# TensorE's order in an attention stage: from the planner's to one written out tile by tile

## The chip, the core and the metric

The kernel runs on one core of one Trainium2 chip. The metric is the device time of one execution in microseconds (us). A core has TensorE (PE in the rows; its weight loads are PEld), VectorE (DVE), ScalarE (ACT), GpSimd (POOL) and SyncE (SP, which issues nearly all DMAs here). Each engine works through its own instructions in order and waits for others by semaphores.

## What is computed

Clustered attention (2 batches, 8 heads, 768 rows, head size 64) followed by two MLPs over 1536 tokens of width 512, all in float32:

```python
q_assign = argmax(q_n @ c_n.T)      # 16 clusters a head; k_assign likewise
mask = q_assign[:, :, :, None] == k_assign[:, :, None, :]
scores = where(mask, scale * q @ k.T, -1e9)
attn = softmax(scores)
x = (attn @ v), heads side by side  # 1536 x 512
x = silu-like(x @ w_in) @ w_out     # 512 -> 2048 -> 512
out = (sigmoid(x @ w_gate) * (x @ w_val)) @ w_out2   # 512 -> 1536 -> 512
```

## The kernel before

Heads go in pairs p = 0 to 7 (two heads j = 0, 1 in each). A head's 768 query rows are 6 tiles of 128 rows, so a pair has 12 tiles, numbered 0 to 11 here (tile = 6 j + i). For each tile the kernel does the following.

- `scores` (L437): four matmuls into a PSUM tile s, two with the values (ka, qa) and two with the masking rows (k, q). DVE then takes the negated row maximum nm (L450) and ACT the exponential e with its row sums (L455). Each s takes two PSUM banks and there are two of them, so the scores of tile n+2 can start only when e of tile n is done.
- `transposes` (L463): six 128 x 128 transposes of e. Two go into u, which two tiles share and DVE copies once for two tiles (L475); four go into t (L478), copied by DVE for even and by ACT for odd tiles (L480). All copies land in one SBUF ring ph. The PSUM pool for u and t, `ps_t`, has three banks and also serves pm, ps, pt and pr below.
- `values` (L482): for each group of three tiles, twelve matmuls v over the ring with 64-column weights (L486), which run in two column halves of the array. ACT copies one half (`other`, L495) and DVE adds it to the other (`xf`, L498). A pair has groups 0 to 3 (tiles 0-2, 3-5, 6-8, 9-11).

Beside this, `prep(p + 1)` (L368) makes the next pair ready in eight pieces, one at each `yield`: 1 POOL scales and splits q; 2 POOL splits k, twelve DMAs place the parts, PE makes the cluster products pm (L151, 32-column weights), ACT scales them; 3 PE transposes them (ps, L162), ACT copies; 4 DVE maximum (L406); 5, 6 DVE compares and weighs (L409, L412); 7 DVE L414 and L416 (oh); 8 PE transposes oh (pt, L425), ACT writes `rows` (L427), four DMAs carry them into the masking rows of the next pair (L429, L430). For pair 0, `first_masks` (L335) stands ahead of it with three pieces of its own, the last with a pt at L319. `finish(p)` (L500) normalizes a finished pair: DVE adds and inverts the sums (L504, L506), PE transposes them (pr, L508), ACT copies (L510); in later steps two DMAs spread them over the partitions (L576 to L579), POOL multiplies (acc, L516), and after pair 3 POOL goes on to make operands of the first MLP (L530, L65, L75). The last pair ends with `finish_last` (L552).

The order of the work in attention comes from the loop at L594: at step n it traces the values of the group that ended with tile n - 4, the scores of tile n + 2, pieces of prep, and the transposes of tile n. All engines are then placed by the framework's planner (outside of `manual_schedule` blocks), which may move an instruction ahead of others by its own estimates. Only the start of the kernel (`first`, L179) and TensorE's order in the MLPs (`order`) are written out by hand:

```python
LOOK, LAG = 2, 4
for n in range(len(tiles) + LAG):
    if n >= LAG: ... values(pp_, jj, ii // GT)
    if n < len(tiles): ... scores(*tiles[n + LOOK]); next(nxt, None); transposes(p, j, i)
```

During the last pair, weights for the first MLP are converted from two 32-bit words (`converted`, L649): ACT L658, POOL L659, DVE L664, L666, L668, each DVE step behind one of the last pair's row maxima.

Of the kernel before, what the change touches and what calls it, by code (L numbers as in the profile page):

```python
# [31 lines left out]
def clustered_attention_then_two_mlps(ctx, tc, qT, kT, v, cen, cenT, w1i, w1o, w2g, w2v, w2o, out):  # L32
    nc = tc.nc
    B, HP, _, S = qT.shape
# [4 lines left out]
    NT = S // P  # L39
# [5 lines left out]
    NPAIR = B * HP  # L45
# [3 lines left out]
    GT = G // P  # L49
# [8 lines left out]
    maxima = []  # L58
# [49 lines left out]
    with ExitStack() as att:  # L108
# [19 lines left out]
        def after_masks(p):  # L128

            return tc.issue_after(masked[p].ins) if p in masked else nullcontext()  # L130

        def load(p):
            b, hp = divmod(p, HP)
            qq = raw.tile([P, S], F32, tag="qq", name=f"qq{p}")
            kk = raw.tile([P, S], F32, tag="kk", name=f"kk{p}")
            vv = hd[p % 2].tile([P, 2, NT, D], F32, tag="vv", name=f"vv{p}")
            with after_masks(p - 1):
                nc.sync.dma_start(qq, qT[b, hp])
                nc.sync.dma_start(kk, kT[b, hp])
                loaded[:] = [nc.sync.dma_start(vv, v[b, hp])]  # L140
            raws[p] = (qq, kk, vv)
# [176 lines left out]
        def choice_rows(pt, j, i, at):  # L318
            nc.tensor.transpose(pt[0:D, at * P : (at + 1) * P], oh[0][:, i, j].rearrange("p n c -> p (n c)"), identb)  # L319
# [15 lines left out]
        def first_masks():  # L335
            yield from first_choice(1, sums)
            pt = ps_t.tile([P, 1024], BF16, tag="t", name="pt0_1")
            for i in range(NT):
                choice_rows(pt, 1, i, i)
            query_rows(1, pt, 0, 0, NT // 2)  # L340
            key_rows(nc.vector, 1, pt, 0, 0, NT)
            query_rows(1, pt, NT // 2, NT // 2, NT // 2)
            yield
# [7 lines left out]
        with tc.issue_after(cast(nc.gpsimd, mine, chosen.pop()).ins):  # L351
            with tc.issue_after(zeros(0, 1).ins):
                late = nc.gpsimd.tensor_tensor(km[U, 1], kk[U], kh[U], op=ALU.subtract)
# [83 lines left out]
        def scores(p, j, i):  # L437
            qa, qm, ka, km, _ = heads[p]
            s = ps_s.tile([P, 2, 512], F32, tag="s", name=f"s{p}_{j}_{i}")
            for n, (a, c) in enumerate(((qa, ka), (qm, km))):  # L440
                for g in range(2):
                    nc.tensor.matmul(  # L442
                        s[:, g, 0:HS],
                        lhsT=a[:, j, i * P : (i + 1) * P],
                        rhs=c[:, j, g * HS : (g + 1) * HS],
                        start=n == 0,
                        stop=n == 1,
                    )
            nm = sm.tile([P, 1], F32, tag="nm", name=f"nm{p}_{j}_{i}")
            maxima.append(nc.vector.tensor_reduce(nm, s[:, :, 0:HS], axis=AX.XY, op=ALU.max, negate=True))  # L450
            e = wk.tile([P, 2, HS], F32, tag="e", name=f"e{p}_{j}_{i}", bufs=4)
            if p not in tots:
                tots[p] = fin.tile([P, 2 * NT], F32, tag="tot", name=f"tot{p}")
            n = j * NT + i
            x = nc.scalar.activation(e, s[:, :, 0:HS], AF.Exp, bias=nm, scale=1.0, accum_out=tots[p][:, n : n + 1])  # L455
            if (p, j, i) == (NPAIR - 1, 0, 0):
                begin.append(x)
            prob[p, j, i] = e
# [4 lines left out]
        def transposes(p, j, i):  # L463
            e = prob.pop((p, j, i)).rearrange("p a b -> p (a b)")
            if i % 2 == 0:
                shared[0] = ps_t.tile([P, 2, 2, P], F32, tag="t", name=f"u{p}_{j}_{i}")
            both = shared[0]
            for kt in (4, 5):
                nc.tensor.transpose(both[:, kt - 4, i % 2, :], e[:, kt * P : (kt + 1) * P], ident)  # L469
            if i % 2:  # L470
                cast(
                    nc.vector,
                    ring[:, 4:6, (i - 1) * P : (i + 1) * P],
                    both.rearrange("p k i q -> p k (i q)"),
                )  # L475
            t = ps_t.tile([P, 4, P], F32, tag="t", name=f"t{p}_{j}_{i}")
            for kt in range(4):
                nc.tensor.transpose(t[:, kt, :], e[:, kt * P : (kt + 1) * P], ident)  # L478
            eng = nc.scalar if i % 2 or (p == NPAIR - 1 and i) else nc.vector
            cast(eng, ring[:, 0:4, i * P : (i + 1) * P], t)  # L480

        def values(p, j, g):  # L482
            vv = heads[p][4]
            o = ps_v.tile([P, G], F32, tag="v", name=f"v{p}_{j}_{g}")
            for n, kt in enumerate((4, 5, 0, 1, 2, 3)):
                m = nc.tensor.matmul(  # L486
                    o[(L, U)[kt % 2]],
                    lhsT=vv[:, j, kt, :],
                    rhs=ring[:, kt, g * G : (g + 1) * G],
                    start=n < 2,  # L490
                    stop=n >= NT - 2,
                )
            main, rest = (L, U) if j == 0 else (U, L)
            other = wk.tile([P, G], F32, tag="other", name=f"other{p}_{j}_{g}", bufs=1)
            ends[:] = [nc.scalar.activation(other[main], o[rest], AF.Copy), m]  # L495
            if p not in xf:
                xf[p] = fin.tile([P, S], F32, tag="xf", name=f"xf{p}")
            nc.vector.tensor_tensor(xf[p][main, g * G : (g + 1) * G], o[main], other[main], op=ALU.add)  # L498
# [53 lines left out]
        def finish_last(h):  # L552

            p = NPAIR - 1
            b, hp = divmod(p, HP)
            n = NT // 2
            t = tots[p].rearrange("p (j i) -> p j i", j=2)[:, :, h * n : (h + 1) * n]
            nc.vector.tensor_scalar_add(t, t, 1e-9)
            rs = fin.tile([P, 2, n], F32, tag="rs", name=f"rs{p}_{h}")
            nc.vector.reciprocal(rs, t)  # L560
            rb = ps_t.tile([P, 512], F32, tag="t", name=f"rb{p}_{h}")
            for j, r in enumerate((L, U)):
                for i in range(n):
                    nc.tensor.matmul(
                        rb[r, i * P : (i + 1) * P],
                        lhsT=rs[:, j, i : i + 1].to_broadcast([P, D]),
                        rhs=ident,
                        start=True,
                        stop=True,
                    )  # L570
            nc.vector.tensor_tensor(
                acc[:, hp, h, b, :], xf[p][:, h * HS : (h + 1) * HS], rb[:, 0:HS], op=ALU.mult
            )
# [7 lines left out]
        if NPAIR > 1:  # L581
            load(1)
        tiles = [(p, j, i) for p in range(NPAIR) for j in range(2) for i in range(NT)]
        LOOK, LAG = 2, 4
        for t in tiles[:LOOK]:
            scores(*t)
        warm(WARM[3])
        first.__exit__(None, None, None)
# [2 lines left out]
            zeros(1, 1)  # L591

        work = []
        for n in range(len(tiles) + LAG):  # L594
            if n >= LAG:
                pp_, jj, ii = tiles[n - LAG]
                if ii % GT == GT - 1:
                    values(pp_, jj, ii // GT)
            if n < len(tiles):
                p, j, i = tiles[n]  # L600
                later = tc.issue_after(maxima[1].ins) if n < 6 else nullcontext()
                if (j, i) == (0, 0):
                    nxt = prep(p + 1) if p + 1 < NPAIR else iter(())
                    if p == 0:
                        nxt = chain(first_masks(), nxt)
                if n + LOOK < len(tiles):
                    t = tiles[n + LOOK]
                    if t[1:] == (0, 0):
                        for _ in nxt:
                            pass  # L610
                        if p + 2 < NPAIR:
                            load(p + 2)
                    scores(*t)
                with later:
                    next(nxt, None)
                    if n < 6:
                        next(nxt, None)
                transposes(p, j, i)
            if n >= LAG:
                if pp_ == NPAIR - 1:  # L620
                    if jj == 1 and ii in (NT // 2, NT - 1):
                        finish_last(ii // (NT // 2 + 1))
                elif (jj, ii) == (1, NT - 1):
                    work.append(finish(pp_))
            work = [w for w in work if next(w, work) is not work]
        for w in work:
            for _ in w:
                pass


    wp = ctx.enter_context(tc.tile_pool(name="wp", bufs=3))
# [491 lines left out]
```

## Time and profile before

Times of whole executions and the page's busy times:

| what | us |
|---|---|
| median of 3 runs | 786.36 (785.64 to 789.41) |
| the profiled execution | 785.58 |
| its span, first to last instruction | 783.9 |
| PE busy in the span | 766.0 (98%) |
| DVE busy | 633.1 (81%) |
| ACT busy | 394.2 (50%) |
| POOL busy | 399.4 (51%) |
| granted TensorE clock | 1.000 of full speed |

The span holds the attention stage (to about 245 us), then the two MLPs. Busy PE is not PE at its peak: matmuls overlap, and the ends of matmuls are modelled, so distances between starts say more than durations. In a timeline row the number in square brackets is idle time before the instruction and what ended it.

### The profile page before, as it was taken

The numbers are of one execution on the slowest core, as the hardware profiler recorded it, in microseconds if no ns is written. First come the engines' busy times: TensorE is split into PE (matmuls) and PEld (weight loads), VectorE is DVE, ScalarE is ACT, GpSimd is POOL, SyncE is SP. The second block draws the span as 40 slices with busy tenths as digits, with TensorE's granted clock in tenths as the row PEclk, the third lists the DMA queues.
The fourth block names the chain that finished last, engine by engine and source line by source line (L and its number), as shares of the span: only waits on it lengthen the run. The fifth ranks groups of instructions, "written<-read, shape, count | busy, mean of one in ns | idle before, by whom it ended". The sixth has DMA issues, their size and how long they took to land.

```text
span 783.9 us, 11429 instructions
## 1 busy us (share of the span) xinstructions
PE 766.0 (98%) x4314; PEld 655.3 (84%) x4314; DVE 633.1 (81%) x803; ACT 394.2 (50%) x674; POOL 399.4 (51%) x345
## 2 busy tenths in 40 slices
PE   8999999999989999999999999999999999999998
PEld 4666766777757998989989989998998989999896
DVE  7786987887886989978688678998497896979746
ACT  6666766666767755525425236546532425333220
POOL 5324123457565756746446326445664846848220
PEclk9999999999999999999999999999999999999999
DMA  7764566467321132221221121211121221111004
GB/s 214 177 160 122 144 162 148 116 162 183 95 74 55 54 108 97 93 80 64 72 81 55 60 75 54 81 57 61 45 82 54 81 81 54 54 67 69 1 0 161
DMA packets 25487, 71.60 MB, mean 91 GB/s; under 512 B 4484, under 2 KB 4952, under 8 KB 25432
## 3 DMA queue, kind: packets, MB, share of 16 engines
q1 hardware_dynamic: 24888, 70.84, 30.3%
q8 instruction: 34, 0.56, 0.3%
q14 instruction: 21, 0.17, 0.1%
q10 hardware_dynamic: 544, 0.03, 0.0%
HBM read 48.01 MB, written 3.19 MB: 65 GB/s over the span
## 4 chain that ended last, share of the span: by engine, by line
PE 83%; DVE 7%; DMA 3%; ACT 3%; issue 2%; POOL 1%; SPq 0%; POOLq 0%; ACTq 0%; DVEq 0%
PE z L947 12%; PE v L486 7%; PE s L442 7%; PE h_0x L773 4%; PE t L478 4%; PE h_0w L773 4%; PE y L888 3%; PE g_0w L773 3%; PE g_0x L773 2%; PE v_0w L773 2%; PE v_0x L773 2%; PE y_00None L888 2%; PE r L838 2%; PE q L838 2%; PE y_01None L888 2%; PE y_20None L888 2%
## 5 line engine op out<-in xcount | busy, mean ns | idle before, releaser
L455 ACT ACTIVATE e<-s,nm 128x768 f32<-128x768 f32 x96 | 86.4, 900 | 38.5 <-DVE nm L450 36.2
L450 DVE TENSOR_REDUCE nm<-s 128x1 f32<-128x768 f32 x96 | 90.7, 948 | 6.8 <-PE s L442 5.4
L947 PE MATMUL z<-wu,ghb 128*128 128x512 f32 (+1 forms) x292 | 89.6, 388 | 0.4 <-DVE acc L868 0.4
L486 PE MATMUL v<-ph,vv 128*64 128x384 f32 x384 | 70.3, 496 | 1.4 <-DVE ph L66 1.4
L947 PEld LDWEIGHTS z<-wu,ghb 128*128 128x128 f32 x292 | 54.1, 188 | 12.3 <-issue 1.2
L442 PE MATMUL s<-ka,qa 128*128 128x384 f32 x192 | 58.0, 383 | 6.4 <-ACT e L455 5.7
L478 PE MATMUL t<-ident,e 128*128 128x128 f32 x384 | 58.1, 275 | 0.2
L947 PE MATMUL z<-wu,glb 128*128 128x512 f32 (+1 forms) x146 | 56.9, 390 | 0.0
L516 POOL TENSOR_TENSOR acc<-xf,rb 128x768 f32<-128x768 f32 x7 | 13.6, 1938 | 80.7 <-DMA rb<-d_rb 68.4
L442 PEld LDWEIGHTS s<-ka,qa 128*128 128x128 f32 x192 | 28.9, 189 | 26.5 <-ACT e L455 15.0
L486 PEld LDWEIGHTS v<-ph,vv 128*64 128x64 f32 x384 | 24.7, 136 | 31.0 <-issue 26.2
L442 PE MATMUL s<-k,q 128*128 128x384 f32 x192 | 49.9, 339 | 0.0
L478 PEld LDWEIGHTS t<-ident,e 128*128 128x128 f32 x384 | 43.6, 140 | 7.0 <-issue 4.2
L868 DVE TENSOR_TENSOR acc<-z,acc 128x1024 f32<-128x1024 f32 (+2 forms) x32 | 36.5, 1152 | 13.5 <-PE z L947 12.9
L498 DVE TENSOR_TENSOR xf<-v,other 64x384 f32<-64x384 f32 x32 | 17.7, 555 | 34.3 <-ACT other L495 34.2
L63 ACT ACTIVATE ph<-t 128x512 f32<-128x512 f32 x52 | 31.0, 597 | 20.3 <-PE t L478 19.9
L469 PE MATMUL u<-ident,e 128*128 128x128 f32 x192 | 36.5, 274 | 0.1
L442 PEld LDWEIGHTS s<-k,q 128*128 128x128 f32 x192 | 34.8, 188 | 0.8 <-issue 0.6
L676 POOL TENSOR_TENSOR wo<-co,wo 128x512 fp32r<-128x512 f32 x16 | 23.4, 1461 | 19.4 <-ACT wo L63 19.2
L947 PEld LDWEIGHTS z<-wu,glb 128*128 128x128 f32 x146 | 27.4, 188 | 7.0 <-DVE glb L828 1.4
L66 DVE COPY ph<-u 128x512 f32<-128x512 f32 x48 | 32.6, 679 | 0.8 <-PE u L469 0.8
L888 PE MATMUL y<-gha,wo 128*128 128x384 f32 x128 | 32.8, 334 | 0.0
(626 smaller groups left out, 2153.7 us busy)
## 6 DMA issues: line engine op xcount, KB each, us to landing
ri<-in_w1i SPq DMA_DIRECT2D x16, 512.0 KB, 3.2
ro<-in_w1o SPq DMA_DIRECT2D x16, 512.0 KB, 3.2
ka<-kh SPq DMA_DIRECT2D x32, 192.0 KB, 3.9
rg<-in_w2g SPq DMA_DIRECT2D x12, 512.0 KB, 3.1
rv<-in_w2v SPq DMA_DIRECT2D x12, 512.0 KB, 3.2
ru<-in_w2o SPq DMA_DIRECT2D x12, 512.0 KB, 3.2
qq<-in_qT SPq DMA_DIRECT2D x8, 384.0 KB, 3.3
kk<-in_kT SPq DMA_DIRECT2D x8, 384.0 KB, 4.7
```

Source lines behind the costliest of these rows:

```text
L66: return nc.vector.tensor_copy(o, i)
L442: nc.tensor.matmul(s[:, g, 0:HS], lhsT=a[:, j, i * P : (i + 1) * P], rhs=c[:, j, g * HS : (g + 1) * HS], start=n == 0, stop=n == 1,)
L450: maxima.append(nc.vector.tensor_reduce(nm, s[:, :, 0:HS], axis=AX.XY, op=ALU.max, negate=True))
L455: x = nc.scalar.activation(e, s[:, :, 0:HS], AF.Exp, bias=nm, scale=1.0, accum_out=tots[p][:, n : n + 1])
L469: nc.tensor.transpose(both[:, kt - 4, i % 2, :], e[:, kt * P : (kt + 1) * P], ident)
L478: nc.tensor.transpose(t[:, kt, :], e[:, kt * P : (kt + 1) * P], ident)
L486: m = nc.tensor.matmul(o[(L, U)[kt % 2]], lhsT=vv[:, j, kt, :], rhs=ring[:, kt, g * G : (g + 1) * G], start=n < 2, stop=n >= NT - 2,)
L773: nc.tensor.matmul(o[:, b, 0:HS], lhsT=w[a][s][:, k, :], rhs=right[b, q][t][:, k, :], start=start and k == 0 and n == 0, stop=k == KQ - 1 ...
L838: nc.tensor.matmul(o[:, h, 0:HS], lhsT=w[f"a{m + 1}{r + 1}"][s][:, k, :], rhs=right[b, f"{r + 1}{h + 1}"][t][:, k, :], start=r == 0 and k ...
L868: nc.vector.tensor_tensor(z, o, z, op=ALU.add)
L888: nc.tensor.matmul(o[:, d, 0:width], lhsT=s[:, d, k, :], rhs=t[:, c], start=k == 0 and m == 0, stop=k == 1 and m == 2,)
L947: nc.tensor.matmul(o[:, a, c], lhsT=s[:, q * P : (q + 1) * P], rhs=r[:, c], start=k == 0 and m == 0, stop=k == 1 and m == 2, skip_group_ch ...
```

## The change

TensorE alone gets a hand-written order from pair 0's tile 0 to the last pair's tile 9 (a `manual_schedule` block for PE); the other engines stay with the planner. In each step the scores of tile i + 2 come first. At every third tile (2, 5, 8, 11) a value group follows, the one that ended three tiles earlier: group 3 of the pair before at tile 2, groups 0, 1 and 2 at tiles 5, 8 and 11. Then come the pieces due early, the transposes of tile i, the pieces due late, and one step of `finish`. `PIECES` says how many pieces stand before and behind the transposes of each tile. The last two tiles' transposes and the last two value groups lie behind the block.

```diff
-        LOOK, LAG = 2, 4
...
-        for n in range(len(tiles) + LAG):
...
+        def finishing(n):
+            for _ in range(n):
+                work[:] = [w for w in work if next(w, work) is not work]
+        def pieces(n):
+            for _ in range(n):
+                next(nxt, None)
+        def gated_start(p, n):
+            return tc.issue_after(maxima[1].ins) if p == 0 and n < 6 else nullcontext()
+        def due(p, n):
+            p, n = (p, n) if n >= 0 else (p - 1, n + 4)
+            if p >= 0:
+                values(p, n // 2, n % 2)
+                if n == 3:
+                    work.append(finish(p))
+        PIECES = (
+            ((2, 0), (0, 0), (1, 1), (1, 0), (1, 1), (0, 1), (0, 1), (0, 1), (1, 0), (0, 0), (0, 0), (0, 0)),
+            ((0, 0), (1, 0), (1, 1), (0, 1), (0, 1), (0, 1), (0, 0), (1, 0), (0, 0), (0, 0), (0, 0), (0, 0)),
+        )
+        def one_tile(p, i, fresh):
+            if i == 2 * NT - 2:
+                pieces(99)
+                if p + 2 < NPAIR:
+                    load(p + 2)
+            elif i == 0 and p:
+                pieces(1)
+            scores(*fresh)
+            early, late = PIECES[min(p, 1)][i]
+            with gated_start(p, i):
+                if i % GT == GT - 1:
+                    due(p, i // GT - 1)
+                pieces(early)
+                transposes(p, *divmod(i, NT))
+                pieces(late)
+                finishing(1)
+        steady = tc.manual_schedule(engines={mybir.EngineType.PE})
+        steady.__enter__()
+        for p in range(NPAIR):
+            nxt = prep(p + 1) if p + 1 < NPAIR else iter(())
+            if p == 0:
+                nxt = chain(first_masks(), nxt)
+            for i in range(2 * NT if p + 1 < NPAIR else 2 * NT - 2):
+                one_tile(p, i, tiles[p * 2 * NT + i + 2])
+        steady.__exit__(None, None, None)
+        finishing(99)
+        for i in (NT - 2, NT - 1):
+            transposes(p, 1, i)
+        for g in range(2):
+            values(p, 1, g)
+            finish_last(g)
```

## Rows read from the trace of the kernel before

**Rows 1.** Stretches (pair 0, 3, 7): us, busy PE, PEld, DVE, ACT, POOL, clock, DMA, GB/s

```profile
14.33:43.85 29.52, 27.25 (x179) 19.05 (x180) 24.72 (x40) 18.89 (x39) 13.13 (x14) 1.00 0.70 185
...
100.73:129.07 28.34, 27.89 (x189) 19.98 (x188) 23.51 (x36) 19.11 (x38) 7.49 (x7) 1.00 0.57 144
...
214.11:244.58 30.47, 26.13 (x164) 17.83 (x163) 25.82 (x40) 22.09 (x45) 21.89 (x19) 1.00 0.20 66
```

**Rows 2.** Timeline of PE in pair 3: start us, us, instruction, [idle before <-releaser]

```profile
101.73 0.60 PE L478 MATMUL t<-ident,e 128*128 128x128 f32 x4
102.33 0.48 PE L151 MATMUL pm<-qq,cc 128*32 128x384 f32 x1
...
103.11 2.16 PE L486 MATMUL v<-ph,vv 128*64 128x384 f32 x12
...
111.11 0.60 PE L478 MATMUL t<-ident,e 128*128 128x128 f32 x4
111.64 2.16 PE L486 MATMUL v<-ph,vv 128*64 128x384 f32 x12
113.72 0.62 PE L442 MATMUL s<-ka,qa 128*128 128x384 f32 x2
...
114.76 0.60 PE L478 MATMUL t<-ident,e 128*128 128x128 f32 x4
115.11 0.59 PE L442 MATMUL s<-ka,qa 128*128 128x384 f32 x2
...
115.89 0.38 PE L469 MATMUL u<-ident,e 128*128 128x128 f32 x2
116.11 0.60 PE L478 MATMUL t<-ident,e 128*128 128x128 f32 x4
117.07 0.62 PE L442 MATMUL s<-ka,qa 128*128 128x384 f32 x2 [0.36 <-ACT e L455]
...
123.38 0.60 PE L478 MATMUL t<-ident,e 128*128 128x128 f32 x4
124.05 0.62 PE L442 MATMUL s<-ka,qa 128*128 128x384 f32 x2
```

**Rows 3.** Timeline of all engines in pair 4: scores of tile 7 to scores of tile 9

```profile
142.07 0.62 PE L442 MATMUL s<-ka,qa 128*128 128x384 f32 x2
...
142.53 0.52 PE L442 MATMUL s<-k,q 128*128 128x384 f32 x2
...
143.34 0.94 DVE L450 TENSOR_REDUCE nm<-s 128x1 f32<-128x768 f32 x1
...
145.42 0.62 PE L442 MATMUL s<-ka,qa 128*128 128x384 f32 x2 [0.36 <-ACT e L455]
```

**Rows 4.** Timeline of PE in pair 0: scores and, right behind them, values

```profile
32.35 0.60 PE L442 MATMUL s<-ka,qa 128*128 128x384 f32 x2
...
33.22 0.87 PE L486 MATMUL v<-ph,vv 128*64 128x384 f32 x4
```

**Rows 5.** Timeline of PE in pair 0; then two lines of tile rows

```profile
20.18 0.51 PE L151 MATMUL pm<-qq,cc 128*32 128x384 f32 x1 [0.67 <-POOL qq L381]
...
31.20 0.51 PE L425 MATMUL pt<-identb,oh 128*128 128x128 bf16 x6 [0.82 <-DVE oh L416]
...
L429 SPq DMA_DIRECT2D k<-rows x7: 507/580/587, 34.0 to 206.1; - x7
...
DMA to landing us min/median/max: 2.1/2.1/2.2
```

**Rows 6.** Timelines of POOL and DVE in pairs 6 and 7

```profile
205.09 1.83 POOL L516 TENSOR_TENSOR acc<-xf,rb 128x768 f32<-128x768 f32 x1 [12.27 <-DVE ph L66]
...
217.51 0.82 DVE L664 TENSOR_SCALAR ci<-ci 128x512 int32<-128x512 int32 x1 [1.50 <-POOL ci L659]
```

**Rows 7.** DVE's groups in pairs 2 to 6: busy us, mean ns | idle before <-releaser

```profile
L498 DVE TENSOR_TENSOR xf<-v,other 64x384 f32<-64x384 f32 x19 | 10.5, 555 | 23.1 <-ACT other L495 23.1
L66 DVE COPY ph<-t 128x512 f32<-128x512 f32 x30 | 20.3, 678 | 0.0
```

More of the change, by code (lines that the diff above doesn't have):

```diff
@@ L583, in clustered_attention_then_two_mlps @@
         tiles = [(p, j, i) for p in range(NPAIR) for j in range(2) for i in range(NT)]
-        LOOK, LAG = 2, 4
-        for t in tiles[:LOOK]:
+        for t in tiles[:2]:
             scores(*t)
@@ L593, in clustered_attention_then_two_mlps @@
         work = []
-        for n in range(len(tiles) + LAG):
[L595 to L625, printed above, removed]
@@ L626, in clustered_attention_then_two_mlps @@
-        for w in work:
-            for _ in w:
-                pass
+        def finishing(n):
[12 more added lines that the diff above has]
+                    work.append(finish(p))
```

## The prediction

> **What bounds the kernel now.** I read the stretches first, one for each pair, then TensorE's timeline inside a steady pair, then the engines on which its idle time hangs. Pairs 2 to 6 are alike to 0.02 us; of these five rows the one of pair 3 stands: 28.34 us, PE busy 27.89, DVE 23.51, ACT 19.11 [rows 1]. Pair 0 takes 29.52 and pair 7 30.47, with PE busy less and DVE more [rows 1]. So attention is close to TensorE's bound in the middle, with DVE at 83% right behind it, and it is not at that bound at both ends. The granted clock is 1.00 in all of these stretches [rows 1], so clock is not in question. The MLPs behind run on an order of their own that the diff doesn't touch; I cost them at nothing, because PE works there without a break and would merely start earlier or later.
>
> Inside a steady pair the start-to-start distances give the prices [rows 2]: scores 0.78 (115.11 to 115.89), u 0.22, t 0.35 (114.76 to 115.11), so a tile costs 1.35; a value group 2.08 (111.64 to 113.72); pm 0.78. Beyond these prices there are two kinds of loss. The first is a change of the tiling of the array: t takes 0.53 ahead of a value group instead of 0.35, so 0.18, and 0.60 ahead of pm, so 0.25. The second is the wait for e: t of tile 6 takes 0.96 up to the scores of tile 9 (0.61 lost), t of tile 9 takes 0.67 up to the scores of tile 12 (0.32 lost).
>
> The second kind has a plain cause. Scores of tile n+2 need the s bank of tile n, which means nm on DVE and then e on ACT. From the start of scores 7 to the start of scores 9 this takes 3.35 us [rows 3]; of that, nm started 0.29 late (the scores end at 143.05, nm starts at 143.34, when DVE comes free). The bare chain is 3.06. PE has only two tiles of work for that time, 2 x 1.35 = 2.70. Wherever a value group or pm lies between, the chain is hidden; where nothing does, PE loses 0.36 at least.
>
> **The change, part by part.** First, the planner's order in a steady pair is already scores n+2, u n, t n. So the matrix work stays the same, and what moves are four value groups, pm, ps, pt and pr.
>
> *Value groups.* In the trace they stand behind t 4, ahead of t 7, behind t 10 and behind pm. By hand they stand behind scores 4, 7, 10 and 13, evenly. Count the windows "scores n to scores n+2": a group behind scores i+2 covers the windows of tiles i+1 and i+2, so four groups cover eight of twelve. Of the other four, the window of tile 2 has pm in it and that of tile 8 has pt; those of tiles 5 and 11 have nothing. Before, too, two were bare (7 and 10). So the waits don't vanish, they move: minus 0.61 and 0.32, plus twice between 0.36 and 1.3. The upper end is 0.36 plus one more DVE copy (0.68) and part of an xf in front of nm [rows 7]. I take 0.50, between the two that are seen, since in both bare windows an xf stands in DVE's queue just before nm, as happened with nm 7 [rows 3]. Sum: +0.07.
>
> *Changes of tiling.* Removed: twice 0.18 and once 0.25 = 0.61 [rows 2]. Added: the only value group right behind scores in the trace stretches these from 0.78 to 0.87 [rows 4], so 4 x 0.09 = 0.36. The way out of a group lies inside its 2.08. pm now stands alone between scores and u instead of directly ahead of a group: one way in and one way out more, unseen in this place. Nearest rows: 0.09 and 0.25 for the way in; below it could be nothing. I take 0.20. Sum: -0.05. TensorEngine Tiling (Array Packing) of the Trainium skill, section Key Properties, says that changing the tiling mode drains TensorE; it speaks against pm on its own. Charged at the dearest row, 0.25 both in and out, pm would cost 0.50 instead of 0.20, 2 us over six pairs, and the time would come out at 786. The trace agrees that a change costs something, but not one sum for all: pm to v, also a change, shows no loss (0.78).
>
> *pr, ps, pt.* pr moves from behind t 3 to behind t 2. There it can wait for DVE's reciprocal or for the bank that ps held: 0 to 0.3, no row shows it; set against the like small waits around ps now, nothing.
>
> So a steady pair changes by +0.02, nothing, between -0.6 (bare chain, pm free: 0.72 + 0.36 - 0.93 - 0.61 = -0.46, and the small waits gone) and +1.7 (both waits at 1.3, pm at 0.5: 2.6 + 0.36 + 0.5 - 0.93 - 0.61 = 1.9, less the small waits). Pairs 1 to 6: 0.0.
>
> *Pair 0.* Here pm stands behind t 1 and waits for POOL until 20.18, and pt waits 0.82 for oh [rows 5]. By hand, scores 5 no longer stand behind pm. From pm at 20.3, with the prices above: pm, u 3 and t 3 end at 21.7; scores 6, ps (three transposes, taken as 0.3), u 4 and t 4 at 23.3; scores 7, group 0 and tile 5 at 26.8; tiles 6 and 7 with one bare window at 30.0; scores 10 and group 1 at 33.0. Then comes pt, later than now. It has a string behind it: pt at 31.20, the k row DMA issued at 34.0, landed 2.1 later [rows 5], so 4.9 us until the next pair's scores can start: 37.9. PE has pt (taken like a t, 0.4), u 8, t 8 and tile 9 for it, 2.3 us, and then waits 2.6. Behind it come scores 12, tile 10, scores 13, group 2 and tile 11, 0.78 + 0.57 + 0.78 + 2.17 + 0.57 = 4.9, so 42.8 against 43.85 where pair 0's stretch ends. I take -0.9 of these 1.05, for DVE's queue; bounds -2.5 (pt early enough, no wait) and +1 (pt a tile later).
>
> *Last pair.* DVE is busy 25.82 of 30.47 [rows 1] and holds PE up. 1.50 us of its idle time is a wait for POOL's ci, with nm queued behind it [rows 6]. POOL is late because it sat idle for 12.27 us until 205.09 and worked without a break after that [rows 6]; the row names a DVE copy as its releaser, but the last operand of this product is rb, the spread row sums of pair 5, and the chain of waits runs through their DMA. Those sums start at pr, which now comes one tile earlier (1.35). So that wait shrinks by 1.35 to 1.50; I take -1.5. What is late next is DVE itself. The planner lays DVE's queue anew, though, so -4 to +3.
>
> Sum: 0.0 - 0.9 - 1.5 = -2.4. The profiled execution, 785.58, is 0.78 below the median of 786.36; against the median this is 784.0.
>
> **The rivals.**
>
> *DVE has room* (faster). DVE idles 1.22 us ahead of each xf (23.1 over 19) [rows 7]: the group stands ahead of scores, so during its 2.08 us DVE has no new s. By hand scores stand ahead of the group and nm runs beside it. If this clears DVE's queue, both waits fall to the bare 0.36 and the small waits go: -0.6 for six pairs = -3.6; pair 0 -2.0; in the last pair the 1.50 [rows 6] and as much again of the 4.65 us in which DVE idles there (30.47 - 25.82) [rows 1], -3.0. Total -8.6: 777.8. Against it: DVE's five steps of prep (L406 to L416) now fall into tiles 2 to 5, next to the bare window of tile 5.
>
> *nm comes too late at tile 5* (slower). Between group 3 and scores 5 the change stacks xf (0.56), the copy of t 2 (0.68) [rows 7], the maximum over ps, the sums and their reciprocal for pr. If the planner puts a copy and a DVE step, 1.2 us, ahead of nm 5, the bare window of tile 5 costs 1.2 more: six pairs +7.2, less 0.9, 792.7. It decides over the forecast's gain from 0.4 us a pair. VectorE's queue is strictly first in, first out by TensorE: Matmul & The Clock Gate of the Trainium skill (its table of specifications); the trace, with nm 0.29 late [rows 3], agrees. For: the chain has no slack there. Against: ps stands behind the group, which leaves DVE 2 us.
>
> *Nothing changes.* The planner's order was nearly this one, and pair 0 and the tail come out as now: 786.4.
>
> **How the numbers follow.** Even middle with gains at the ends (784.0): 0.40. DVE has room (777.8): 0.30. nm late (792.7): 0.15. Nothing: 0.15. A measurement of this kernel tells about 0.5%, 3.9 us, from no change: 782.4 to 790.3. Faster takes the second case and a quarter of the first, 0.40; slower takes most of the third and a little of the tail's spread, 0.17; same is the rest, 0.43. The range 777 to 790 takes in the second case and leaves out most of the third and the outermost part of the second.
>
> **What would show it.** Right: pairs at 28.0 to 28.6 us, waits for e ahead of scores 7 and 13 of 0.3 to 0.7 each and none ahead of scores 9; scores ahead of v at 0.87; in pair 0 a wait for the rows DMA ahead of scores 12; no POOL wait of 1.5 in the last pair. Wrong: pairs under 27.9 (DVE had room) or above 29 with nm behind other DVE steps; a last pair that is shorter or longer than 30.47 by over 3 us would be the planner's doing on DVE and would decide the sign alone.

## The result, and the profile after

The changed kernel takes 792.97 us (median of five runs, 791.71 to 794.72), the kernel before 787.45 beside it (five runs). The ratio is 1.0074 with a 95% interval of 1.005 to 1.0099: slower, by 0.5% to 1.0%. The profiled execution takes 791.71 against 785.58, the span 789.9 against 783.9: +6.0 us. One execution of run n below took 2276.94 us, at a granted clock of 1.000, and its ratio leaves it out.

The stretches come first, cut as in [rows 1], from the scores of tile 2 of one pair to those of the next; the last line runs from there in pair 7 to the first product p behind attention (L859; 41.00 us before). Columns: us, busy time of PE, PEld, DVE, ACT, POOL, granted clock, DMA share, GB/s.

```profile
14.59:44.43 29.84, 26.54 (x180) 19.01 (x180) 23.93 (x40) 19.49 (x39) 10.02 (x12) 1.00 0.62 168
102.49:131.52 29.03, 27.86 (x190) 19.42 (x188) 23.36 (x36) 19.01 (x39) 7.75 (x7) 1.00 0.57 143
218.60:261.23 42.63, 36.06 (x236) 26.00 (x235) 33.49 (x48) 28.09 (x54) 21.87 (x21) 1.00 0.18 59
```

Against [rows 1], pair 0 is 0.32 longer and the steady pair 0.69, with nearly the same busy time on PE (27.86 for 27.89) and DVE (23.36 for 23.51): what grew is idle time. The six pairs 1 to 6 give +3.91, the last stretch +1.63, an earlier or later start +0.26, the MLPs nothing (525.49 against 525.48 from the first p to the end of DVE's last step). The sum is +6.1, against +6.0 in the span. The clock is 1.00 in all three, so it has no part in this profile.

PE's waits over the whole span (us in total, times, longest):

```profile
PE s L442 <- ACT e L455: 9.8, 15, 3.1
PE t L478 <- DVE ph L66: 2.6, 7, 1.5
PE s L442 <- DMA k<-rows: 2.2, 1, 2.2
```

Before, the first read 5.7 us in 14 waits, 0.7 at most. Now inside a steady pair (pair 4, PE's timeline: start, us, instruction, idle time and releaser), from the transposes of tile 2 to group 0 and on to tile 7:

```profile
138.73 0.60 PE L478 MATMUL t<-ident,e 128*128 128x128 f32 x4
139.35 0.28 PE L508 MATMUL pr<-ident,rs 128*12 128x128 f32 x1
139.38 0.59 PE L442 MATMUL s<-ka,qa 128*128 128x384 f32 x2
139.81 0.52 PE L442 MATMUL s<-k,q 128*128 128x384 f32 x2
...
141.74 0.60 PE L478 MATMUL t<-ident,e 128*128 128x128 f32 x4
143.09 0.61 PE L442 MATMUL s<-ka,qa 128*128 128x384 f32 x2 [0.75 <-ACT e L455]
...
143.98 2.16 PE L486 MATMUL v<-ph,vv 128*64 128x384 f32 x12
...
149.19 0.39 PE L469 MATMUL u<-ident,e 128*128 128x128 f32 x2
149.75 0.66 PE L478 MATMUL t<-ident,e 128*128 128x128 f32 x4 [0.17 <-DVE ph L66]
```

From t of tile 4 to scores 7 it is 1.35 instead of 0.35: 1.00 lost in the bare window of tile 5. The releaser is e, but e waits for nm, and nm stands here (DVE's timeline, same pair):

```profile
138.81 0.56 DVE L498 TENSOR_TENSOR xf<-v,other 64x384 f32<-64x384 f32 x1 [1.71 <-ACT other L495]
139.41 0.55 DVE L406 TENSOR_REDUCE mk<-sim 128x24 f32<-128x384 f32 x1
139.99 0.69 DVE L66 COPY ph<-t 128x512 f32<-128x512 f32 x1
140.60 0.55 DVE L409 TENSOR_TENSOR eq<-sim,mk 128x384 bf16<-128x384 f32 x1
141.07 0.95 DVE L450 TENSOR_REDUCE nm<-s 128x1 f32<-128x768 f32 x1
```

Scores 5 end at 140.33 (139.81 and 0.52); nm starts 0.74 later, behind xf, the maximum, a copy and eq. Of these only xf and the copy are due; eq leads to the next pair's masks, which TensorE needs only for pt, behind scores 9.

Three more losses of the steady pair: t 10 to scores 13 takes 0.81 (0.46 lost), u 7 to t 7 0.56 instead of 0.22 (0.34: pt holds one of the three banks, and t 7 must wait for the copy of t 6), t 2 to pr 0.62 instead of 0.35 (0.27). What pr waits for is the bank that ps held; ACT's copy of ps frees it, ending at 139.30 (ACT's timeline, same pair), and the profile names this copy as the releaser of pr in six of seven pairs:

```profile
138.81 0.49 ACT L63 ACTIVATE sim<-ps 128x384 f32<-128x384 f32 x1
```

With 0.06 behind t 7 the waits come to 2.13; the same reading of [rows 2] and its neighbours gives 1.39 before. The tiling changes went the other way, about 0.70 after 0.86. That makes +0.58 of the +0.69; the rest is spread too thinly for my reading to place.

### The profile page after: what moved, and what is told of

The parts are those of the page before. It is cut to its first block, busy times and chain, and to the rows that moved or that the text cites. A ratio compares the mean times of both kernels' runs of the same rounds, so it can differ in the third digit from the quotient of the medians.

```text
span 789.9 us, 11440 instructions
## 1 busy us (share of the span) xinstructions
PE 763.6 (97%) x4313; PEld 651.5 (82%) x4314; DVE 636.3 (81%) x803; ACT 395.4 (50%) x674; POOL 397.4 (50%) x345
## 4 chain that ended last, share of the span: by engine, by line
PE 78%; DVE 12%; ACT 4%; issue 2%; POOL 2%; DMA 1%; SPq 0%; ACTq 0%; POOLq 0%; DVEq 0%
PE z L968 12%; PE v L486 7%; PE s L442 5%; PE h_0x L794 4%; PE h_0w L794 3%; PE y L909 3%; PE g_0w L794 3%; DVE nm L450 3%; PE t L478 3%; PE g_0x L794 2%; PE v_0w L794 2%; PE v_0x L794 2%; PE y_00None L909 2%; PE r L859 2%; PE q L859 2%
## 5 line engine op out<-in xcount | busy, mean ns | idle before, releaser
L469 PEld LDWEIGHTS u<-ident,e 128*128 128x128 f32 x192 | 23.5, 141 | 22.0 <-issue 17.5
L469 PE MATMUL u<-ident,e 128*128 128x128 f32 x192 | 38.4, 281 | 1.5 <-ACT e L455 1.3
```

## The experiments

Fourteen kernels ran, in five groups (a to d; e, f, h; i to l; m; n and o), each with the kernel before on the same chip. That kernel's median was 786.09 to 786.98 there, so across groups it is the ratios that compare, not the medians. "Middle" is a stretch of pairs 2 to 6, "last" the last stretch, "scores 11" how long after the start of the last stretch the scores of tile 11 start. All three and pair 0 are from the profiles, us; the ratio is from the runs.

| run | median | ratio to before (95%) | pair 0 | middle | scores 11 | last |
|---|---|---|---|---|---|---|
| before | 787.45 | | 29.52 | 28.34 | 24.55 | 41.00 |
| the change | 792.97 | 1.0074 (1.005, 1.0099) | 29.84 | 29.03 | 24.99 | 42.63 |
| a old places by hand | 790.04 | 1.0048 (1.0033, 1.0063) | 29.90 | 28.37 | 26.82* | 43.41* |
| b last pair, group first | 791.59 | 1.0075 (1.005, 1.0099) | 29.88 | 29.03 | 22.56 | 40.20 |
| c pair 0, pt earlier | 789.18 | 1.0042 (1.0027, 1.0057) | 27.56 | 29.03 | 24.97 | 42.87 |
| d t 2 copied by ACT | 790.64 | 1.0061 (1.0044, 1.0078) | 31.18* | 28.55 | 24.43 | 42.04 |
| e no bare window | 794.73 | 1.0103 (1.0086, 1.012) | 30.49 | 29.51 | 23.20 | 40.80 |
| f ends by hand, old middle | 786.79 | 0.9995 (0.9983, 1.0007) | 27.56 | 28.35 | 24.74 | 43.95* |
| h change, both ends mended | 788.65 | 1.0018 (1.0008, 1.0028) | 27.88 | 29.03 | 22.90 | 41.03 |
| i change, weights later | 792.27 | 1.0069 (1.0052, 1.0086) | 31.37* | 29.02 | 23.42 | 42.65* |
| j before, weights later | 784.64 | 0.9978 (0.9969, 0.9986) | 29.17 | 28.35 | 24.17 | 40.42 |
| k spread behind copies | 785.78 | 0.9985 (0.9976, 0.9994) | 28.13 | 28.40 | 26.07* | 42.22* |
| l = f, weights later | 784.41 | 0.9965 (0.9953, 0.9977) | 27.54 | 28.36 | 23.16 | 42.61* |
| m = l, last pair to planner | 782.57 | 0.9948 (0.9935, 0.9962) | 27.54 | 28.37 | 23.04 | 39.49 |
| n = m, the change's middle | 787.15 | 0.9999 (0.9989, 1.0009) | 27.54 | 29.04 | 21.33 | 38.98 |
| o = i, group between last tiles | 790.98 | 1.006 (1.0038, 1.0081) | 29.88 | 29.03 | 22.68 | 40.99 |

A star marks a stretch in which the granted clock fell to 0.50 for some microseconds; its length mixes the order's cost with the clock's (in a and k the fall came ahead of scores 11). What stands behind the stars is told under i.

**The middle: a, d, e, k.** Run a keeps the order written out by hand but puts groups, pm, ps and pr of pairs 1 to 7 where the planner had them.

```diff
-            ((0, 0), (1, 0), (1, 1), (0, 1), (0, 1), (0, 1), (0, 0), (1, 0), (0, 0), (0, 0), (0, 0), (0, 0)),
+            ((0, 1), (0, 0), (1, 0), (0, 1), (0, 1), (0, 1), (0, 1), (1, 0), (0, 0), (0, 0), (0, 0), (0, 0)),
...
-                if i % GT == GT - 1:
+                if p == 0 and i % GT == GT - 1:
...
+                if p and i == 7:
+                    due(p, 1)
                 transposes(p, *divmod(i, NT))
                 pieces(late)
+                if p and i in (0, 4, 10):
+                    due(p, {0: -1, 4: 0, 10: 2}[i])
+                if i == 3:
+                    work.extend(held)
+                    held.clear()
```

The list `held` keeps `finish`, and so pr, back until tile 3.

> TensorE's order is still written by hand, but in pairs 1 to 7 the groups, pm, ps and pr stand where the planner of before had put them (only u 7 now follows pt and its group). Theory: what costs time in the middle is where the groups stand, so the stretch from tile 2 of one pair to tile 2 of the next goes back from 29.03 to 28.3 us, the wait ahead of scores 7 (1.00) is gone and the one ahead of scores 9 (0.6) is back; 6 x 0.69 = 4 us off the change's time, 789 or a little less. Rival: a fixed order as such costs time, because the other engines are planned around it; then the stretch stays at 29.0 and the time at 793.

The middle is back at 28.37 (only pair 3 takes 28.72), and the old wait ahead of scores 9 with it: 0.94 from t 6, 0.59 lost (PE's timeline, pair 4):

```profile
144.97 0.60 PE L478 MATMUL t<-ident,e 128*128 128x128 f32 x4
145.91 0.62 PE L442 MATMUL s<-ka,qa 128*128 128x384 f32 x2 [0.35 <-ACT e L455]
```

So the middle's loss comes from the places, not from the order being fixed. The total stays high through the ends, which a did not mend.

Run d takes one step out of DVE's queue ahead of nm 5: tile 2's copy goes to ACT.

```diff
-            eng = nc.scalar if i % 2 or (p == NPAIR - 1 and i) else nc.vector
+            eng = nc.scalar if i % 2 or (p == NPAIR - 1 and i) or (j, i) == (0, 2) else nc.vector
```

> The change with TensorE's order as it is, but ACT instead of DVE copies t of tile 2 in each pair. DVE's queue is otherwise the same. Theory: nm 5 starts 0.69 us late because the copy of t 2 and eq stand ahead of it; without the copy it is 0.1 late, the wait ahead of scores 7 falls from 1.00 to 0.4 us, a pair takes 28.4 and the time falls by 3.6 us to 789.4. Rival: the tile changes between scores, groups and transposes and the place of the groups cost the time, DVE's queue does not; then a pair stays at 28.9 to 29.0 and the time at 792 to 793.

DVE's timeline and then PE's, pair 4:

```profile
139.23 0.55 DVE L406 TENSOR_REDUCE mk<-sim 128x24 f32<-128x384 f32 x1
139.82 0.56 DVE L409 TENSOR_TENSOR eq<-sim,mk 128x384 bf16<-128x384 f32 x1
140.41 0.96 DVE L450 TENSOR_REDUCE nm<-s 128x1 f32<-128x768 f32 x1
```

```profile
139.21 0.59 PE L442 MATMUL s<-ka,qa 128*128 128x384 f32 x2
...
142.44 0.61 PE L442 MATMUL s<-ka,qa 128*128 128x384 f32 x2 [0.29 <-ACT e L455]
```

nm 5 is now 0.26 late instead of 0.74, the wait loses 0.53 instead of 1.00, and the pair is 0.48 shorter. That shows the queue in front of nm 5 to be the larger part of the loss. 28.55 is not yet 28.34, and the bare windows are not what is left: the two lose 0.53 and 0.46 here, the two of the kernel before 0.61 and 0.32. The waits of pr and t 7 stand in d as in the change (0.28 and 0.34). The time, 790.64, misses the 789.4 expected; the clock in pair 0 (the star) took some 1.3 of it.

Run e tried to have no bare window at all: groups at tiles 2, 4, 8 and 10, pm and pt a tile earlier (with b's and c's edits below).

```diff
-            ((0, 0), (1, 0), (1, 1), (0, 1), (0, 1), (0, 1), (0, 0), (1, 0), (0, 0), (0, 0), (0, 0), (0, 0)),
+            ((1, 0), (0, 0), (1, 1), (0, 1), (0, 1), (0, 1), (1, 0), (0, 0), (0, 0), (0, 0), (0, 0), (0, 0)),
...
-                if i % GT == GT - 1:
-                    due(p, i // GT - 1)
+                if i in (2, 4, 8, 10) and (p, i) != (NPAIR - 1, 2):
+                    due(p, {2: -1, 4: 0, 8: 1, 10: 2}[i])
```

> By hand, with the groups and prep's products spread so that something stands between the scores of every second tile: pm behind scores 2, group 3 behind scores 4, group 0 behind scores 6, pt behind scores 8, group 1 behind scores 10, group 2 behind scores 12; pair 0 and the last pair as in the two runs that mended them. Theory: the waits for e sit in the windows from scores n to scores n+2 that hold no other work, so with none bare they are under 0.2 us each, a pair takes 27.4 to 27.7 us, and the time is about 779, faster than both kernels. Rival: DVE's queue is the bound in the middle (23.2 us of work in fixed order, chained to e), and the waits only move; then a pair stays at 28.2 to 28.6 and the time is 783 to 786.

A miss: 29.51, the longest middle of all. PE's and DVE's timelines show where the wait went:

```profile
115.39 2.16 PE L486 MATMUL v<-ph,vv 128*64 128x384 f32 x12 [0.91 <-DVE ph L66]
```

```profile
113.33 0.55 DVE L409 TENSOR_TENSOR eq<-sim,mk 128x384 bf16<-128x384 f32 x1
113.79 0.95 DVE L450 TENSOR_REDUCE nm<-s 128x1 f32<-128x768 f32 x1
114.66 0.68 DVE L66 COPY ph<-u 128x512 f32<-128x512 f32 x1
```

Group 0, a tile earlier, needs the u copy that tiles 2 and 3 share, and that stands behind nm; 1.07 is lost there, 0.68 ahead of group 2 and 0.51 ahead of pr. Run k, with groups 0 and 2 behind those copies (the ends as in l), gave most of this back:

```diff
+                if p in (0, NPAIR - 1):
...
+                elif i in (2, 8):
+                    due(p, {2: -1, 8: 1}[i])
                 pieces(early)
                 transposes(p, *divmod(i, NT))
                 pieces(late)
+                if 0 < p < NPAIR - 1 and i in (4, 10):
+                    due(p, {4: 0, 10: 2}[i])
```

> Hand-written ends, loads later, and in pairs 1 to 6 something in every window again, but groups 0 and 2 behind the transposes of tiles 4 and 10 instead of ahead of them (the shared u copies of tiles 2, 3 and 8, 9 are then done), pr behind t 3. Theory: groups 0 and 2 lost 0.9 and 0.5 us to these copies in the run without a bare window; now a pair takes 27.8 to 28.2 us, and the time is 780 to 782. Rival: DVE's queue keeps a pair at 28.3 or above; 783 or more.

28.40, no better than the planner's places: ahead of group 0 PE still waits 0.24 for a copy, and t takes 0.73 ahead of scores 10 and 0.68 ahead of pr, instead of 0.35. The rival held. Neither of these two spreads beats the planner's places. That DVE's queue would do the same to any other is argued, not shown.

**Pair 0: c.** pt moves from early in tile 8 to late in tile 7.

```diff
-            ((2, 0), (0, 0), (1, 1), (1, 0), (1, 1), (0, 1), (0, 1), (0, 1), (1, 0), (0, 0), (0, 0), (0, 0)),
+            ((2, 0), (0, 0), (1, 1), (1, 0), (1, 1), (0, 1), (0, 1), (1, 1), (0, 0), (0, 0), (0, 0), (0, 0)),
```

> The change, but in pair 0 pt stands behind tile 7's transposes instead of behind group 1, some 3 us earlier. Theory: the wait of 2.2 us ahead of scores 12 for the rows DMA goes, and the time falls by 2.2 us to 790.8; the middle stays at 29.03 us a pair. Rival: pt then waits for oh on DVE by as much, or the other DMAs of the next pair are what is late, and less than 0.7 us is saved.

In the change, the next pair's masking rows hold scores 12 up (PE's timeline of the change, then of c):

```profile
36.99 0.60 PE L442 MATMUL s<-ka,qa 128*128 128x384 f32 x2
39.80 0.63 PE L442 MATMUL s<-k,q 128*128 128x384 f32 x2 [2.21 <-DMA k<-rows]
```

```profile
31.68 0.49 PE L425 MATMUL pt<-identb,oh 128*128 128x128 bf16 x6
...
37.10 0.60 PE L442 MATMUL s<-ka,qa 128*128 128x384 f32 x2
37.53 0.51 PE L442 MATMUL s<-k,q 128*128 128x384 f32 x2
```

In the change pt starts at 34.71 and the rows are there 5.1 us later; in c it starts 3.0 earlier (31.68), the wait is gone, and the stretch is 2.28 shorter.

**The last pair: b, f, h.** Run b puts group 3 of pair 6 ahead of scores 4 of pair 7 again, where PE can work on it while it waits.

```diff
+            if p == NPAIR - 1 and i == 2:
+                due(p, -1)
             scores(*fresh)
```

> The change, but in the last pair group 3 of pair 6 stands ahead of scores 4 instead of behind them. Theory: PE's wait of 3.07 us there (nm 2 behind DVE's step ci, which waits for POOL) was exposed because the group stood behind the scores that wait; the group's 2.1 us now fill it, and the time falls by 2 us to 791. Rival: DVE sets the last pair's length whatever PE does, PE waits 2 us more a little later, and the time stays at 793.

What it works against is this (the change, PE's timeline, then DVE's):

```profile
224.63 0.62 PE L442 MATMUL s<-ka,qa 128*128 128x384 f32 x2 [3.07 <-ACT e L455]
...
225.53 2.16 PE L486 MATMUL v<-ph,vv 128*64 128x384 f32 x12
```

```profile
221.74 0.82 DVE L685 TENSOR_SCALAR ci<-ci 128x512 int32<-128x512 int32 x1 [2.01 <-POOL ci L680]
222.59 0.96 DVE L450 TENSOR_REDUCE nm<-s 128x1 f32<-128x768 f32 x1
```

DVE stands 2.01 us for POOL's ci with nm 2 behind it, so scores 4 wait 3.07, and the group, which needs none of this, is fixed behind them. With the group in front the last stretch is 2.4 shorter and the profiled execution 2.1 (789.63). The ratio does not move: the other three executions of b have mean clocks of 0.995 to 0.997, so the gain is shown by the profiles alone. Two runs put edits together: f (b's and c's edits with a's middle) and h (the change with b's and c's).

```diff
-                if i % GT == GT - 1:
+                if p in (0, NPAIR - 1) and i % GT == GT - 1 and (p, i) != (NPAIR - 1, 2):
...
+                if 0 < p < NPAIR - 1 and i == 7:
+                    due(p, 1)
...
+                if 0 < p < NPAIR - 1 and i in (0, 4, 10):
+                    due(p, {0: -1, 4: 0, 10: 2}[i])
```

> By hand with the planner's old places in pairs 1 to 6, pair 0's pt early and group 3 first in the last pair. Theory: the stretches add up: pair 0 at 27.6 us, the middle at 28.35 a pair, the last stretch at 40.2 to 40.8, so 2 to 3 us below the time before, 783 to 784. Rival: the stretches hang together through the planner and the DMA queue, and the time stays within 1 us of the time before, 786.

> The change with both mended ends (pair 0's pt early, group 3 first in the last pair) and its own middle. Theory: the middle alone is left as a loss, 6 x 0.69 = 4.1 us, against gains of 2.0 in pair 0 and 0.8 in the last stretch: 787 to 788, 1 to 2 us above the time before. Rival: the mended ends do not add, and it stays at 790 or above.

h came out at 788.65, near what the parts gave. f is level with before, as its rival had it, and its last stretch went against me: POOL's ci came at 3.48 after the start of the last stretch (h 1.57, b 1.11), scores 11 at 24.74 (22.90, 22.56), nearly us for us. The trace says why ci is late: pr has its old place in f, so d_rb goes out 18.11 ahead of the last stretch (h 19.45), and rb follows it by 5.79 (5.25); together 1.88 of the 1.91. So the last stretch hangs on when POOL comes to ci.

**The weights' DMAs: i, j, l.** SP's queue in the change (its timeline: start, us, issue):

```profile
197.38 1.50 SPq L674 DMA_DIRECT2D ri<-in_w1i  x2
198.98 0.34 SPq L577 DMA_DIRECT2D d_rb<-rt  x1
205.02 1.11 SPq L579 DMA_DIRECT2D rb<-d_rb  x2
```

The row sums of pair 5 (d_rb, 6 KB) go out right behind two 512 KB loads of MLP weights, and rb, which must read them back, can be issued only 6.04 us later (4.96 before). POOL's chain to ci starts at rb. In i, j and l (and in k, m, n and o) those loads are issued behind rb:

```diff
+                last = nc.sync.dma_start(rb[r], d[j : j + 1, :].to_broadcast([D, S]))
+            if rb.name.startswith(f"rb{NPAIR - 3}"):
+                loaded[:] = [last]
```

> The change, but SP issues the first two weight loads of the MLP (ri, 512 KB each) behind the two rb DMAs of pair 5 instead of right ahead of its d_rb. Theory: d_rb needs 6 us there because it stands behind these loads; without them 1.3 to 2 us, so POOL's ci ends some 4 us earlier, DVE's wait of 2.01 us for it is gone, PE's wait ahead of scores 4 of the last pair falls from 3.07 to under 0.7 us and the last stretch from 42.6 to about 40 us: 790 to 791. Rival: the small DMA is slow for another reason or DVE's work sets the last stretch; it stays at 42 us or above and the time at 792 to 793.

> The kernel before, with the same two loads behind the rb DMAs of pair 5. Theory: POOL's ci comes 3.5 us earlier, DVE's wait of 1.50 us goes, and the last stretch falls from 41.0 to 39.5, the time by 1 to 1.5 us. Rival: the planner had filled that wait with the group, nothing is gained, within 0.5 us of the time before.

> The run with hand-written ends and the old places in the middle, with the same two loads later. Theory: its last stretch of 43.95 us is long because POOL's ci came 2.4 us later than in the run with the group first; with the loads out of the way it falls to 40 to 40.5, and the time to 783, 3 to 4 us below the time before. Rival: its last stretch hangs on something else and stays above 42; 785 to 787.

In i, d_rb to rb takes 3.14 (not the 1.3 to 2 expected), in j 2.68; in i DVE no longer waits for ci, and PE's wait ahead of scores 4 is 1.35 instead of 3.07 (under 0.7 was expected). j gains 0.2% on the kernel before, l 0.3% on f; l's last stretch misses its 40 to 40.5, with the clock at 0.50 in it. In i the last stretch seems not to move (42.65), as the rival had it. The timeline says otherwise: scores 11 come 1.57 earlier than in the change, u of tile 11 still 1.42 earlier (27.83 after the start of the stretch against 29.25). Then the clock falls, and the last tile takes longer by just that. PE's timeline of i, from u of tile 11:

```profile
248.03 0.69 PE L469 MATMUL u<-ident,e 128*128 128x128 f32 x2 [1.31 <-ACT e L455]
248.37 2.27 PE L796 MATMUL h_0x<-x,wi0a 128*128 128x384 f32 x6
250.44 1.05 PE L478 MATMUL t<-ident,e 128*128 128x128 f32 x4
```

t takes 1.05 instead of 0.60 [rows 2] and h_0x 2.27 where o, below, shows 1.28. Without the fall the stretch would be about 41.2 (42.65 less 1.42), an estimate. So the theory held to tile 11 with some 1.4 of the 2.6 us that it forecast, and the clock hid that. Among the executions, the one of i at a mean clock of 1.000 took 790.49, the one of the change 791.71.

**The last pair left to the planner: m.** As l, but the hand-written order ends with pair 6; TensorE's order in pair 7 is then that of the kernel before.

```diff
-        for p in range(NPAIR):
+        for p in range(NPAIR - 1):
...
+        p = NPAIR - 1
+        for i in range(2 * NT + 4):
...
+            if i and g % GT == GT - 1:
+                q = p - (i < 4)
+                values(q, g // NT, g % NT // GT)
+            if i + 2 < 2 * NT:
+                scores(*tiles[p * 2 * NT + i + 2])
+            if i < 2 * NT:
+                transposes(p, *divmod(i, NT))
...
```

> Pair 0 and the middle by hand as in the run with hand-written ends (pt early, old places), the weight loads later, and the last pair left to the planner, which orders TensorE there just as in the kernel before. Theory: the hand-written order is what lengthens the last stretch, because its fixed places meet DVE's queue of conversions; with the planner's order it is 40.4 us as in the run of the kernel before with later loads, pair 0 is 27.6, the middle 28.35 a pair, and the time is about 783, 2 us under that run's and 4 under the time before. Rival: the last stretch depends on the timing of the DMAs and not on the order; it stays at 42 or above, and the time at 784.5 or more.

782.57, all five runs within 0.56 us: 0.5% faster than before, the best of all versions. Not all of its gain on l is the order: l's last stretch has the fall of the clock in it, and l's four executions at a mean clock of 1.000 took 782.87 to 784.34. Windows of a steady pair and of its last stretch:

```profile
99.24:127.61 28.37, 27.89 (x189) 19.88 (x188) 23.51 (x36) 19.11 (x38) 7.61 (x7) 1.00 0.57 145
212.72:252.21 39.49, 36.23 (x236) 26.47 (x235) 31.09 (x49) 28.20 (x55) 22.13 (x20) 1.00 0.19 64
```

**Two runs for what was open: n, o.** n is m with the change's places in pairs 1 to 6.

> The fastest version so far (pair 0 with pt a tile earlier, weight loads behind rb, last pair left to the planner), but with the change's places of the value groups, pm, ps and pr in pairs 1 to 6. Theory (the bare window of tile 5 and the small bank waits cost 0.67 us a pair, wherever the ends stand): pairs 1 to 6 at 29.0 again, pair 0 27.5 and the last stretch 39.5 as there, so 6 x 0.67 = 4 us on top of 782.6: 786.5 to 786.9, with the granted clock at 1.00 throughout. Rival (the middle hands DVE over to the last pair in another state): a last stretch over 40.5 or under 38.5, and a time outside 785.5 to 788.

```profile
100.05:129.10 29.05, 27.88 (x189) 19.40 (x188) 23.31 (x36) 19.00 (x39) 7.71 (x7) 1.00 0.57 143
216.21:255.19 38.98, 35.92 (x236) 26.48 (x235) 31.75 (x48) 27.76 (x54) 19.20 (x18) 1.00 0.20 65
```

Pairs 1 to 6 together take 174.23 us against m's 170.06: 4.17 more at full clock, as the theory had it. The median is 787.15, a little above its 786.5 to 786.9; the whole gain of m is lost to the middle.

o adds to i a value group between the last transposes.

```diff
+        transposes(p, 1, NT - 2)
+        values(p, 1, 0)
+        transposes(p, 1, NT - 1)
         steady.__exit__(None, None, None)
...
```

> The change with the weight loads behind rb, and value group 2 of the last pair put by hand between the transposes of tiles 10 and 11 instead of behind both. In the change TensorE waits 1.31 us for e of tile 11 with that group fixed behind it, and from scores 11 to the rb product it takes 8.2 us where the kernel before takes 7.2. Theory (the order behind scores 11 costs this 1 us): 7.1 to 7.4 from scores 11 to rb, so with scores 11 at 23.4 as in the run with the later loads, and 9.4 from rb to the first p product, a last stretch of 40.0 where the clock stays at 1.00; 1 to 2 us less time than with the later loads alone. Rival (DVE's queue sets the end, not TensorE's order): the group or the tile behind it waits for a DVE copy, 8 us or more again, a last stretch of 41 or more, and no gain.

A miss, and not a clean one:

```profile
243.90 0.66 PE L478 MATMUL t<-ident,e 128*128 128x128 f32 x4
245.95 1.28 PE L797 MATMUL h_0x<-x,wi0a 128*128 128x384 f32 x6 [1.40 <-ACT e L455]
247.23 2.16 PE L486 MATMUL v<-ph,vv 128*64 128x384 f32 x12
```

The first MLP product came to stand ahead of the group and took over the wait, 1.40 us; from scores 11 to rb it is 9.0. The clock stayed at 1.00 and the last stretch is 40.99, about what i's would be without its fall. The question it was meant for, PE's order or DVE's queue behind scores 11, stays open in part. The traces do show DVE's queue at work: from scores 11 to the start of nm 11 it is 1.61 in the kernel before and in m, 2.25 in the change and 2.73 in o, in the last two behind a conversion (1.66 and 1.65) and an xf. What TensorE's order would cost there alone, no run shows.

## Why the prediction was wrong, point by point

**The steady pair** was the main error: "+0.02, nothing", measured +0.69. The step that failed is the price of the bare windows, "I take 0.50" for each: their sum, forecast at +0.07, is +0.53 (1.00 and 0.46 for 0.61 and 0.32). For tile 11 it was right (0.46). For tile 5 it measured 1.00, because DVE has three steps besides xf to do between group 3 and nm 5. The bounds of that term, 0.36 to 1.3, held it, but the nearest row that I used, one xf in front of nm, was that of another place in the queue. The second step that failed is pr, ps and pt "set against the like small waits", at nothing: pt costs t 7 its bank (0.34, with 0.06 behind it), and pr waits 0.27 for the bank that ps held. The prediction had named this last wait (0 to 0.3), but not the one for t 7; the small waits come to 0.67 for 0.46, so +0.21. With the tiling changes below that is +0.58; 0.11 is not placed. Over pairs 1 to 6 the loss is +3.91; a and n show that it comes with the places, d that its larger part is DVE's queue.

**The tiling changes** were about right, -0.16 for -0.05. pm on its own costs 0.09 on the way in and 0.05 on the way out, not the 0.20 taken. By the dearest row it would have been 0.50. TensorEngine Tiling (Array Packing) of the Trainium skill, section Key Properties, says that a change of the tiling mode drains TensorE; the trace agrees that a change costs something, but each kind has its own price, here 0.09 and 0.05, against 0.18 and 0.25 behind transposes [rows 2].

**Pair 0**, -0.9 forecast, +0.32 measured. The wait for the rows DMA ahead of scores 12 was foreseen in its place and size (2.21 for 2.6), and the string behind pt too (5.1 for 4.9). What failed is the start of pt, 33.0 by the prices, 34.71 in the trace: the walk had no small waits in it. It lost 0.57 before pm (20.87 for 20.3), 0.40 and 0.31 between u and t of the next two tiles, and the rest in smaller pieces, 1.7 us in all. c shows that one tile decides.

**The last pair**, -1.5 forecast, +1.63 measured. pr did come earlier, counted from the start of its stretch: 1.42 against 1.35. But the step from there to POOL was taken as fixed, and the DMA queue ate most of the gain: rb went out 6.04 us behind d_rb, 4.96 before, and POOL's ci came only 0.27 earlier (2.49 after the start of the last stretch for 2.76). i shows that the term was sound up to tile 11 where the loads don't stand in front (scores 11 at 23.42, 1.13 earlier than before). What I had not costed is that a fixed order puts the wait ahead of work that could fill it; b shows that, 2.4 shorter with the group in front. By the pieces: +0.44 up to scores 11, +1.05 from there to rb (8.21 for 7.16), +0.14 behind.

**The rival that happened** is "nm comes too late at tile 5", 792.7 with a chance of 0.15. Its mechanism is the one in DVE's rows, and d shows it, though eq stands there and not the sums and their reciprocal, which DVE had done 9 us ahead of pr. Its price was 1.2 a pair and is 0.5 to 0.7. That its total fits is luck: the middle gave +3.9 where it had +7.2, and the ends gave +1.95 where it had -0.9. "Against: ps stands behind the group, which leaves DVE 2 us" was the argument that misled me: DVE spends 1.71 of these idle, waiting for ACT's `other`, and its steps come after. "DVE has room" fell: DVE idles less ahead of xf (0.9 us each in pairs 2 to 6, 1.2 before), but nm came later, not earlier, in the window that mattered. "Nothing changes" fell too.

## What to carry to other kernels

A wait that is short in one place does not price the same wait elsewhere: read what stands in the late engine's queue between the release and the step that matters, here the row maximum. Here a fixed order was as good as the planner's in the middle only with the planner's places, and better in pair 0 once its one long wait was out of the way. In the last pair, where POOL, DMA and the next stage's weights come in, two things helped: work that needs nothing put ahead of the instruction that may wait, or the stretch left to the planner. And look at the granted clock of every stretch before two lengths are compared.

## What was not expected of the hardware

**A small DMA behind large ones.** 6 KB from SBUF, issued right behind two 512 KB loads, let its reader go 6.04 us later (4.96 in the kernel before); with the loads moved behind it, 3.14 (2.68). In pairs 0 to 4 of the change, without these loads but behind one of 384 KB, it is 3.10 to 4.46.

**The clock after a wait.** In all six profiles with the change's pair 0, TensorE stands 2.2 us for the rows. In the change, a, b and o it then goes on at full clock. In d and i, with the same order there, the granted clock is 0.50 right after it, the lower of the two levels (1.2 GHz). Windows of d in pair 0, behind the wait, and two lines of its PE timeline:

```profile
37.00:39.19 2.19, 0.00 (x1) 0.00 (x1) 0.92 (x3) 1.10 (x3) 0.00 (x0) 1.00 0.44 81
39.19:40.70 1.51, 1.51 (x9) 1.47 (x9) 0.85 (x1) 0.00 (x0) 0.00 (x0) 0.68 0.79 179
40.70:42.20 1.50, 1.50 (x6) 1.10 (x4) 0.79 (x2) 0.99 (x2) 0.44 (x1) 0.50 0.88 348
```

```profile
39.19 0.62 PE L442 MATMUL s<-k,q 128*128 128x384 f32 x2 [2.25 <-DMA k<-rows]
...
39.97 1.06 PE L478 MATMUL t<-ident,e 128*128 128x128 f32 x4
```

The stretch is then 31.2 to 31.4 instead of 29.9: the wait costs another 1.3 to 1.5. The five runs of the change show the same spread, with mean clocks of 1.000, 0.998, 0.997, 0.995 and 0.995 for 791.71, 792.97, 792.52, 793.9 and 794.72 us; m, without these waits, has 1.000 in all five and spreads by 0.56. So some 1.3 of the change's median (792.97 less the profiled 791.71) goes with the clock, an estimate. It does not explain the ratio: the median of the kernel before, too, lies above its profiled execution (787.45 for 785.58). Why it falls in one execution and not in another, no run here shows.
